# Strassen's seven products for the second feed-forward block's output too

## The chip, the cores and the metric

The kernel runs on one core of a Trainium2 chip. The core has a matrix engine (PE, TensorE; its weight loads are listed as PEld), a vector engine (DVE, VectorE), a scalar engine (ACT, ScalarE), GpSimd (POOL) and SP, which here only issues transfers (DMAs). The engines run their own instruction lists in order and wait for one another through semaphores. The metric is the time on the device in microseconds, of the whole program in one launch.

## The reference, cut to what matters

```
x = chunk_attention(q, k, v, mem_k, mem_v)         # 3072 tokens x 512
h1 = x @ moe_w_in;   g1 = h1 - tanh(h1);   y1 = g1 @ moe_w_out        # 512 -> 2048 -> 512
h2 = y1 @ moe2_w_in
g2 = maximum(h2, 0) + alpha * minimum(h2, 0)
out = g2 @ moe2_w_out                                                 # 3072 x 512, float32
```

The result is float32. Every matrix factor is split into a high part (`fp32r`, rounded) and a low part (the rest), and each product is three matmuls: high x high, high x low, low x high (`PASS` in the code).

## The kernel before, in words

**First layer.** Attention and the first feed-forward block run together, in 6 blocks of 512 tokens. In a block, for each of 16 slices `f` of the 2048 hidden units, PE makes `h` (L241), ACT takes the tanh, DVE subtracts, ACT and POOL split the result (`gh`, `gl`), and PE adds to `y` (L280). Beside this, in blocks 1 to 4 the second layer's weights are prepared ("parked"): one step per slice converts a piece of the weights from float64 to float32, forms what is needed, splits it and writes it to DRAM, to `w2i` for the inner weights and to `w2o` for the outer ones (`park_in`, `park_sum`, `park_out`). The inner weights are already parked as the seven operands of a Strassen product. The pool `w` has 34 tiles of 4 KB per partition; layer 1's own weights hold 32 of them while it runs.

**Second layer.** It runs in 3 blocks of 1024 tokens, each with an h stage and a y stage.
- The **h stage** (`pair_h`, 8 times) makes two slices of `h2` at once by Strassen's seven products in the order 1, 6, 5, 2, 7, 3, 4: 7 products x 6 matmuls of 128x512 (L368). DVE adds the products up (L385), ACT and DVE make `g2` (`prelu`: two ACT copies `n`, then one DVE instruction, L376 to L378).
- The **y stage** (`block_y`, 16 slices) is plain: `g2` is split into `g2h` and `g2l` (ACT, POOL), these are the stationary factors, the columns of `w_out` stream, and eight PSUM banks collect 8 token tiles of 128 x 512: 24 matmuls per slice, 384 per block (L445). Then the eight tiles are copied out by ACT and DVE and stored in rows of 2 KB. Each slice's weights are one load of 512 KB (`load_out`) into the space of layer 1's `ring`.
- In the y stage the next block's inputs are prepared as well (`x2_work`: 4 loads, 4 DVE sums, 7 splits).

The order on each engine is set by a scheduler from the order of the code and the tiles' dependencies. GpSimd does most subtractions that make the low parts, SP issues nearly all DMAs.

## Time and profile before

| | |
|---|---|
| median of 3 timed runs | 1111.22 us (1110.45 to 1113.46) |
| the profiled execution, first to last instruction | 1110.0 us |
| PE busy | 1082.4 us, 98% |
| DVE, ACT, POOL busy | 523.6, 478.4, 426.8 us |
| layer 2: first h stage, first y stage | 63 us and 88 us |

The profiled execution gives its span, 1110.0 us; the timed runs include what lies around the span, and their median is 1.2 us above it. Times below are microseconds from the span's start unless "mean ns" is said. An engine counts as busy while an instruction of it runs; PE runs its matmuls in a pipeline, so their pitch (start to start), not their duration, is what a matmul costs.

### The profile page before, as it was taken

Reading aid. Unit: us, or ns where it says so; the run is one execution under the profiler, and the core shown is the slowest. Engines: PE = TensorE matmul, PEld = TensorE weight load, DVE = VectorE, ACT = ScalarE, POOL = GpSimd, SP = SyncE. Lnnn points to the kernel's source line nnn. Section 1 sums busy time; section 2 is a strip of 40 time slices with the busy share of each in tenths; the row PEclk is TensorE's granted clock in tenths of the full one; section 3 lists DMA queues with packets and bytes.
Section 4 is the critical chain, followed back from the end, with each engine's and each line's share of the span. In section 5 each row is a group of like instructions: output and inputs, shape, how many; then the busy total and the mean of one; then the engine's idle time right before and its main releaser. Section 6 shows DMA issues by size and latency. Waiting matters only on the chain.

```text
span 1110.0 us, 17747 instructions
## 1 busy us (share of the span) xinstructions
PE 1082.4 (98%) x7056; PEld 892.5 (80%) x7056; DVE 523.6 (47%) x875; ACT 478.4 (43%) x789; POOL 426.8 (38%) x279
## 2 busy tenths in 40 slices
PE   4699999999999999999999999999999999999998
PEld 4588888888888888888888888888888888888887
DVE  3688754655646565564311466700566500566000
ACT  3566643443534444443332466520556420557300
POOL 3266633443434343344462000990002990003900
PEclk9699999999999999999999999999999999999999
DMA  9673234554454455335420663543754443751312
GB/s 275 258 265 115 77 124 171 164 147 166 143 176 176 154 162 170 125 148 189 176 67 1 232 214 110 180 164 106 234 194 152 152 161 129 246 175 39 110 43 76
DMA packets 57395, 171.04 MB, mean 154 GB/s; under 512 B 8288, under 2 KB 8544, under 8 KB 57312
## 3 DMA queue, kind: packets, MB, share of 16 engines
q1 hardware_dynamic: 53712, 163.48, 44.1%
q10 hardware_dynamic: 3600, 6.42, 1.6%
q8 instruction: 56, 0.92, 0.3%
q14 instruction: 27, 0.22, 0.1%
HBM read 134.23 MB, written 35.65 MB: 153 GB/s over the span
## 4 chain that ended last, share of the span: by engine, by line
PE 96%; DMA 2%; DVE 1%; issue 1%; POOL 0%; ACT 0%; SPq 0%; ACTq 0%; DVEq 0%; POOLq 0%
PE h L241 24%; PE y L280 24%; PE h L368 20%; PE yb L445 12%; PE y L445 12%; PE pv L609 2%; PE sp L525 2%; PE tp L596 1%; DMA qn<-in_q_dram 1%; DMA ri<-in_moe_w_in_dram 1%; DMA y1d<-ys 0%; PE tp L589 0%; DVE u L102 0%; SPq L495 0%; DVE s L109 0%
## 5 line engine op out<-in xcount | busy, mean ns | idle before, releaser
L241 PE MATMUL h<-ring,wt 128*128 128x512 f32 x1152 | 281.2, 392 | 4.0 <-ACT ring L616 2.2
L241 PEld LDWEIGHTS h<-ring,wt 128*128 128x128 f32 x1152 | 216.9, 189 | 50.7 <-ACT ring L616 2.4
L116 POOL TENSOR_TENSOR g2l<-g,g2h 128x1024 fp32r<-128x1024 f32 x48 | 121.7, 2570 | 282.1 <-ACT g2h L115 282.1
L368 PE MATMUL h<-xh,wi 128*128 128x512 f32 x672 | 209.0, 389 | 0.2 <-DVE g L385 0.2
L280 PE MATMUL y<-gh,wt 128*128 128x512 f32 x768 | 192.7, 391 | 0.0
L266 POOL TENSOR_TENSOR gl<-t,gh 128x512 fp32r<-128x512 f32 x96 | 126.7, 1320 | 155.3 <-ACT gh L265 129.2
L280 PEld LDWEIGHTS y<-gh,wt 128*128 128x128 f32 x768 | 143.2, 188 | 30.4
L368 PEld LDWEIGHTS h<-xh,wi 128*128 128x128 f32 x672 | 126.1, 188 | 27.0 <-DVE g L385 0.6
L257 DVE TENSOR_TENSOR t<-h,t 128x512 f32<-128x512 f32 x96 | 65.7, 685 | 153.6 <-ACT t L256 148.8
L256 ACT ACTIVATE t<-h 128x512 f32<-128x512 f32 x96 | 57.0, 594 | 130.2 <-PE h L241 118.8
L280 PE MATMUL y<-gl,wt 128*128 128x512 f32 x384 | 104.2, 389 | 0.0
L469 DVE COPY ys<-y 128x512 f32<-128x512 f32 x6 | 4.0, 688 | 198.6 <-PE y L445 198.6
L445 PE MATMUL y<-ring,g2h 128*128 128x512 f32 x384 | 96.3, 389 | 0.0
L445 PE MATMUL yb<-ring,g2h 128*128 128x512 f32 x384 | 96.1, 389 | 0.0
L445 PEld LDWEIGHTS y<-ring,g2h 128*128 128x128 f32 x384 | 72.1, 188 | 15.0
L445 PEld LDWEIGHTS yb<-ring,g2h 128*128 128x128 f32 x384 | 72.1, 188 | 15.0
L280 PEld LDWEIGHTS y<-gl,wt 128*128 128x128 f32 x384 | 72.0, 188 | 15.0
L265 ACT ACTIVATE gh<-t 128x512 fp32r<-128x512 f32 x96 | 60.5, 630 | 42.7 <-DVE t L257 34.9
L376 ACT ACTIVATE n<-g 128x512 f32<-128x512 f32 x72 | 45.4, 632 | 72.6 <-DVE g L385 72.2
L368 PE MATMUL h<-xl,wi 128*128 128x512 f32 x192 | 74.7, 389 | 0.0
L378 DVE SCALAR_TENSOR_TENSOR g<-g,n 128x512 f32<-128x512 f32 x72 | 62.7, 870 | 15.8 <-ACT n L377 14.5
L377 ACT ACTIVATE n<-n,alpha_neg 128x512 f32<-128x512 f32 x96 | 67.0, 717 | 1.3
(86 smaller groups left out, 1313.2 us busy)
## 6 DMA issues: line engine op xcount, KB each, us to landing
wi<-w2i SPq DMA_DIRECT2D x72, 512.0 KB, 4.4
ring<-w2o SPq DMA_DIRECT2D x48, 512.0 KB, 3.6
kn<-in_k_dram SPq DMA_DIRECT2D x24, 384.0 KB, 5.1
vn<-in_v_dram SPq DMA_DIRECT2D x24, 384.0 KB, 4.1
ri<-in_moe_w_in_dram SPq DMA_DIRECT2D x16, 512.0 KB, 8.3
ro<-in_moe_w_out_dram SPq DMA_DIRECT2D x16, 512.0 KB, 8.6
pk<-in_moe_w_in_dram SPq DMA_DIRECT2D x16, 512.0 KB, 3.7
w2i<-ws SPq DMA_DIRECT2D x16, 512.0 KB, 2.7
```

What stands on the lines that cost most here:

```text
L116: nc.gpsimd.tensor_tensor(out=lo, in0=v, in1=f32(hi), op=ALU.subtract)
L241: last["ffn"] = nc.tensor.matmul(out=h, lhsT=wi[:, a, kk, :], rhs=ring[c][:, s0:s0 + n, kk, :], start=(i == 0), stop=(i == 3 * KD - 1),).ins
L256: nc.scalar.activation(out=t, in_=h, func=ACTF.Tanh)
L257: last["dve"] = nc.vector.tensor_tensor(out=t, in0=h, in1=t, op=ALU.subtract).ins
L265: nc.scalar.activation(out=gh, in_=t, func=ACTF.Copy)
L266: nc.gpsimd.tensor_tensor(out=gl, in0=t, in1=f32(gh), op=ALU.subtract)
L280: mm = nc.tensor.matmul(out=yp[l, b][j][:, :n * 128], lhsT=wo[:, a, j * 128:(j + 1) * 128], rhs=g[c], start=first, stop=final,)
L368: nc.tensor.matmul(out=h, lhsT=w[:, a, 128 * kt:128 * kt + 128], rhs=x[c][:, kt, :], start=(first and j == 0), stop=(j == 5), skip_group_c ...
L376: nc.scalar.activation(out=n, in_=h, func=ACTF.Relu, scale=-1.0)
L377: nc.scalar.activation(out=n, in_=n, func=ACTF.Copy, scale=alpha_neg[:, f:f + 1])
L378: nc.vector.scalar_tensor_tensor(out=t, in0=h, scalar=0.0, in1=n, op0=ALU.max, op1=ALU.add)
L445: nc.tensor.matmul(out=sets[k][j], lhsT=g[a][:, k, j * 128:(j + 1) * 128], rhs=w[:, c, :], start=(f == 0 and n == 0), stop=(f == NF - 1 an ...
```

## The change

The y stage is made by Strassen's seven products too. Tokens are halved (512 and 512), the hidden units are paired (slices 2p and 2p+1), and the 512 output columns are halved. `w_out` becomes the stationary factor and `g2` streams, so that the products give the output transposed: 128 output columns x 512 tokens in a bank.

- **Parking**: `w_out` is parked as seven operands (`w2o[m]`), columns permuted so that a transpose by 32x32 blocks puts them right. Per pair there are two new sum steps on DVE (`park_out_sum`), and 256 KB stores instead of 512 KB ones.
- **h stage**: after the third result of a pair POOL makes two differences (`t3`, and one in place).
- **y stage**: 7 products x 8 pairs of 6 matmuls (L496 of the changed kernel). `prep` makes one streaming operand: an ACT copy to `fp32r` (L475) and a subtraction on POOL or DVE (L477); product 6 has a DVE sum ahead and one behind. `y_product` issues the matmuls, `y_done` adds the products up and, for four of the seven, transposes 32x32 blocks on DVE and stores 4 x 128 KB in pieces of 256 bytes (128 bytes for the last). The weights of a pair of products are one load of 512 KB, 28 per block instead of 16, in a pool of four tiles that takes the place of `ring`.
- The next block's inputs are prepared later in the y stage.

The diff's core:

```diff
-    w2o = [dr_p.tile([128, 2 * 512], FP32, name=f"w2o{i}") for i in range(NF)]
+    w2o = {m: [dr_p.tile([128, 2 * 2 * 256], FP32, name=f"w2o{m}_{i}") for i in range(NF // 4)]
+           for m in range(1, 8)}
...
+        v = aw.tile([128, 512], FP32, tag="v", name="wv")
+        v = to_f32(raw, v)
+        w = raw.bitcast(FP32R).rearrange("k (a s n) -> k a s n", a=2, s=2)
+        p, odd = divmod(f, 2)
+        sw[odd] = v
+        for k, m in enumerate((2, 4) if odd else (1,)):
+            split_f32(by_column(v[:, 256 * k:256 * k + 256]), by_tile(w[:, 0, k]), by_tile(w[:, 1, k]))
+            park_op(m, p, w[:, :, k])
...
+        s = t_p.tile([128, 512], FP32, tag="t", name="sm")
+        lo, hi = by_tile(s[:, 0:256]), by_tile(s[:, 256:512])
+        if half == 0:
+            nc.vector.tensor_tensor(out=hi, in0=v01, in1=v11, op=ALU.add)
+            nc.vector.tensor_tensor(out=lo, in0=hi, in1=v00, op=ALU.subtract)
+            sw["s2"] = lo
+        else:
+            nc.vector.tensor_tensor(out=lo, in0=v00, in1=v01, op=ALU.subtract)
+            nc.vector.tensor_tensor(out=hi, in0=v10, in1=sw["s2"], op=ALU.subtract)
+        w = w_p.tile([128, 2, 512], FP32R, tag="w", name="ws")
+        split_f32(s, w[:, 0], w[:, 1])
+        for k, m in enumerate((6, 5) if half == 0 else (7, 3)):
+            park_op(m, p, w[:, :, 256 * k:256 * k + 256])
...
+        mi, pp = divmod(i % NO, P2 // 2)
+        w = zr.tile([128, 2, 2, 256], FP32R, tag="wo", name="wo")
+        nc.sync.dma_start(out=f32(w).rearrange("k p a n -> k (p a n)"), in_=w2o[ORDER[mi]][pp])
+        wo2[i] = w
...
+        x = gx[b, p] = w_p.tile([128, 2, 512], FP32, tag="w", name="gx")
+        y = gy[b, p] = w_p.tile([128, 2, 512], FP32, tag="w", name="gy")
+        if p % 2 == 0:
+            t3[b, p // 2] = zr.tile([128, 2, 512], FP32, tag="t3", name="t3")
+        d3 = t3[b, p // 2][:, p % 2]
+        ga, gb = (x[:, 0], y[:, 0]), (y[:, 1], x[:, 1])
...
+        nc.gpsimd.tensor_tensor(out=d3, in0=gb[1], in1=ga[1], op=ALU.subtract)
+        nc.gpsimd.tensor_tensor(out=ga[1], in0=ga[1], in1=ga[0], op=ALU.subtract)
...
+    def y_bank(b, m):
+        if (b % 2 == 0) == (m in (1, 6)):
+            return ps_y.tile([128, 512], FP32, tag="y", name="yb")
+        if m in (1, 5):
+            return ps_h.tile([128, 512], FP32, tag="h", name="yb")
+        return ps_h2.tile([128, 512], FP32, tag="h2", name="yb")
+
+    def prep(b, s):
+        mi, p = divmod(s, P2)
+        m = ORDER[mi]
+        x, y, d3 = gx[b, p], gy[b, p], t3[b, p // 2][:, p % 2]
+        op = w_p.tile([128, 2, 512], FP32R, tag="w", name="go")
+        if m == 6:
+            src = y_bank(b, 7)
+            nc.vector.tensor_tensor(out=src, in0=d3, in1=x[:, 0], op=ALU.add)
+        else:
+            src = {1: x[:, 0], 5: y[:, 0], 2: y[:, 1], 7: d3, 3: x[:, 1], 4: x[:, 0]}[m]
+        nc.scalar.activation(out=op[:, 0], in_=src, func=ACTF.Copy)
+        eng = nc.gpsimd if m == 1 or (m != 6 and p % 4 == 3) else nc.vector
+        eng.tensor_tensor(out=op[:, 1], in0=src, in1=f32(op[:, 0]), op=ALU.subtract)
+        if m == 6:
+            nc.vector.tensor_tensor(out=x[:, 0], in0=y[:, 1], in1=src, op=ALU.subtract)
+        gop[b, s] = op
...
+    def y_product(b, s, tiles=(0, 1)):
+        mi, p = divmod(s, P2)
+        m = ORDER[mi]
+        into = {2: 1, 3: 5, 4: 7}.get(m, m)
+        if m == into and p == 0 and 0 in tiles:
+            yd[b, m] = [y_bank(b, m) for _ in range(2)]
+        w = wo2[b * NO + mi * (P2 // 2) + p // 2][:, p % 2]
+        w = w.rearrange("k a (i n) -> k a i n", i=2)
+        op = gop[b, s]
+        for i in tiles:
+            for n, (a, c) in enumerate(PASS):
                 nc.tensor.matmul(
+                    out=yd[b, into][i], lhsT=w[:, a, i], rhs=op[:, c],
+                    start=(m == into and p == 0 and n == 0), stop=(p == P2 - 1 and n == 2),
+                    skip_group_check=True,
                 )
+
+    def y_done(b, m, tiles=(0, 1)):
+        add = lambda o, p, q: nc.vector.tensor_tensor(out=o, in0=p, in1=q, op=ALU.add)
+        if m in (1, 6, 5):
+            for i in tiles:
+                tag = "gl" if m == 6 else "gh"
+                e = ye[b, m, i] = g_p.tile([128, 512], FP32, tag=tag, name="ye")
+                if m == 1:
+                    nc.scalar.activation(out=e, in_=yd[b, 1][i], func=ACTF.Copy)
+                else:
+                    add(e, yd[b, m][i], ye[b, 1 if m == 6 else 6, i])
             return
+        into, h, t, u = {2: (1, 0, 0, 0), 7: (7, 1, 1, 5), 3: (5, 0, 1, 6), 4: (7, 1, 0, 6)}[m]
+        if 0 in tiles:
+            ye[b, "st"] = w_p.tile([128, 16, 2, 32], FP32, tag="w", name="st")
+        st = ye[b, "st"]
+        for i in tiles:
+            src = yd[b, into][i]
+            if u:
+                c = t_p.tile([128, 512], FP32, tag="t", name="c")
+                add(c, src, ye[b, u, i])
+                src = c
+            nc.vector.transpose(out=st[:, :, i], in_=src.rearrange("k (b n) -> k b n", n=32))
+        t0 = 1024 * b + 512 * t
+        split = len(tiles) == 1
+        for a in range(4):
+            dst = out[t0:t0 + 512, 256 * h + 64 * a:256 * h + 64 * a + 64]
+            dst = dst.rearrange("(b i) (e j) -> i b e j", i=32, e=2)
+            src = st[32 * a:32 * a + 32]
+            if split:
+                dst, src = dst[:, :, tiles[0]], src[:, :, tiles[0]]
+            (nc.scalar if split and a % 2 else nc.sync).dma_start(out=dst, in_=src)
...
+            for s in range(LEAD):
+                prep(b, s)
+            for s in range(7 * P2):
+                if s + LEAD < 7 * P2:
+                    prep(b, s + LEAD)
+                if more or s < 6 * P2:
+                    y_product(b, s)
+                    if s % P2 == P2 - 1:
+                        y_done(b, ORDER[s // P2])
+                    i = b * NO + s // 2 + 4
+                    if s % 2 and i < NB * NO:
+                        load_out(i)
+                if s >= 2 * P2 and s % 2 == 0 and early:
+                    early.pop(0)()
+                if s >= 4 * P2 and late:
+                    late.pop(0)()
+            if not more:
+                for i in range(2):
+                    for p in range(P2):
+                        y_product(b, 6 * P2 + p, (i,))
+                    y_done(b, 4, (i,))
```

How the instructions stand, at three places. **ACT at the end of the first h stage and the start of the y stage, before** (`g_6829` and `g_6830` belong to the last pair; `g2h` is the first y operand):

```order
L376 ACTIVATE n<-h_6831 128x512
L377 ACTIVATE n<-n,alpha_neg 128x512
L115 ACTIVATE g2h<-g_6242 128x1024
L115 ACTIVATE g2h<-g_6243 128x1024
L376 ACTIVATE n<-g_6830 128x512
```

Here one Relu copy and one alpha copy of the last pair stand ahead of the first y operand, a copy of twice the width. The same place on ACT now (`go` is a y operand, made from `gx`; `yb` is a PSUM bank with the sum for product 6; L407 and L408 are `prelu`):

```order
L407 ACTIVATE n<-h_7017 128x512
L407 ACTIVATE n<-gx 128x512
L408 ACTIVATE n<-n,alpha_neg 128x512 x2
L475 ACTIVATE go<-gx 128x512 x8
L475 ACTIVATE go<-yb 128x512
L407 ACTIVATE n<-gy 128x512 x2
L475 ACTIVATE go<-yb 128x512
L408 ACTIVATE n<-n,alpha_neg 128x512 x2
L475 ACTIVATE go<-yb 128x512 x4
```

The first operand copy moved from behind one `n`, alpha copy to behind two of each, and all eight copies for product 1 stand ahead of the first for product 6.

**DVE at the same place now** (L472 is the sum ahead of product 6, L477 the low part of an operand, L479 the difference behind; before, only the last pair's L385 and L378 and four L344 stood here):

```order
L416 TENSOR_TENSOR gy<-h_7054,hu 128x512
L472 TENSOR_TENSOR yb<-t_6408,gx 128x512
L477 TENSOR_TENSOR go<-yb,go 128x512
L479 TENSOR_TENSOR gx<-gy,yb 128x512
L472 TENSOR_TENSOR yb<-t_6607,gx 128x512
L477 TENSOR_TENSOR go<-yb,go 128x512
L479 TENSOR_TENSOR gx<-gy,yb 128x512
L409 SCALAR_TENSOR_TENSOR gy<-gy,n 128x512 x2
```

Up to the last low part for product 6 this goes on in the same manner, 23 DVE instructions from the first L477 of these rows. On POOL eight L477 for product 1 stand in a row, where eight `g2l` of twice the size were mixed with the input splits.

**SP in the first y stage now** (`wo` is a weight tile for two products, `wi` a weight tile of the next h stage, `out_dram` the stores; before, the eight stores of a block stood together at its end):

```order
L353 DMA wo<-w2o_3_116 128x1024
L532 DMA out_dram<-st 32x16x64 x4
L353 DMA wo<-w2o_0_97 128x1024
L361 DMA wi_7546<-w2i_81 128x1024
L361 DMA wi_7557<-w2i_81 128x1024
L361 DMA wi_7570<-w2i_81 128x1024
L353 DMA wo<-w2o_1_98 128x1024
```

Sets of four stores now stand between the weight loads, four sets in each block.

## Rows read from the trace of the kernel before

**Rows 1.** The page's part 1: busy time, share, instructions of each engine.
```profile
PE 1082.4 (98%) x7056; PEld 892.5 (80%) x7056; DVE 523.6 (47%) x875; ACT 478.4 (43%) x789; POOL 426.8 (38%) x279
```

**Rows 2.** Busy time by stage: PE, PEld, DVE, ACT, POOL, granted clock, DMA share, GB/s.
```profile
328.00:424.00 96.00, 96.00 (x778) 78.90 (x778) 55.82 (x106) 42.59 (x78) 39.81 (x33) 1.00 0.49 164
628.40:691.50 63.10, 63.05 (x277) 51.99 (x278) 40.20 (x62) 41.21 (x64) 0.31 (x1) 1.00 0.51 163
691.50:779.90 88.40, 88.40 (x391) 73.19 (x391) 22.41 (x12) 26.66 (x32) 59.26 (x23) 1.00 0.46 155
```

**Rows 3.** The chain that ended last: start, length, what.
```profile
741.82 2.72 PE y L445 x12
...
779.90 74.80 PE h L368 x330
```

**Rows 4.** Groups by line, shapes apart: busy, mean ns of one, idle before.
```profile
L445 PE MATMUL y<-ring,g2h 128*128 128x512 f32 x384 | 96.3, 389 | 0.0
L445 PE MATMUL yb<-ring,g2h 128*128 128x512 f32 x384 | 96.1, 389 | 0.0
L445 PE MATMUL y<-ring,g2l 128*128 128x512 f32 x192 | 52.6, 389 | 0.0
L445 PE MATMUL yb<-ring,g2l 128*128 128x512 f32 x192 | 52.0, 389 | 0.0
L570 DVE STREAM_TRANSPOSE et<-sc 128x512 f32<-128x512 f32 x20 | 14.2, 710 | 23.1 <-POOL sc L563 23.0
```

**Rows 5.** Timelines of ACT, PE, DVE, POOL: start, length, instruction.
```profile
688.80 0.60 ACT L376 ACTIVATE n<-h 128x512 f32<-128x512 f32 x1
690.80 0.68 DVE L385 TENSOR_TENSOR g<-h,hv 128x512 f32<-128x512 f32 x1
691.33 0.85 PE L445 MATMUL y<-ring,g2h 128*128 128x512 f32 x3
691.96 1.14 ACT L376 ACTIVATE n<-g 128x512 f32<-128x512 f32 x2
...
434.18 1.29 POOL L266 TENSOR_TENSOR gl<-t,gh 128x512 fp32r<-128x512 f32 x1
435.43 1.29 POOL L116 TENSOR_TENSOR pk<-wv,pk 128x512 fp32r<-128x512 f32 x1
```

**Rows 6.** Timeline of DVE and POOL in the first y stage.
```profile
708.75 3.42 DVE L344 TENSOR_TENSOR xt<-x,x 128x1024 f32<-128x1024 f32 x1
...
717.73 2.40 POOL L116 TENSOR_TENSOR g2l<-g,g2h 128x1024 fp32r<-128x1024 f32 x1
```

**Rows 7.** One tile's instructions, ns min/median/max: `xt` whole run, `g` first h stage.
```profile
L344 DVE TENSOR_TENSOR xt<-x,x x6: 1215/2424/3423, 539.4 to 871.1; 128x1024 f32<-128x1024 f32 x6
...
L378 DVE SCALAR_TENSOR_TENSOR g<-g,n x21: 682/692/694, 629.0 to 688.7; 128x512 f32<-128x512 f32 x21
```

**Rows 8.** DMA issues by line, whole run: count, KB each, median us to landing.
```profile
ring<-w2o SPq DMA_DIRECT2D x48, 512.0 KB, 3.6
```

**Rows 9.** DMA queue: packets, MB, share of 16 engines; 233.3 to 234.1, then 1106 to 1110.
```profile
q1 hardware_dynamic: 1286, 0.01, 90.1%
...
q1 hardware_dynamic: 547, 0.86, 56.6%
```

**Rows 10.** Timeline of the end: the last matmul, the last copies, the last issue.
```profile
1105.91 0.39 PE L445 MATMUL yb<-ring,g2l 128*128 128x512 f32 x1
1106.34 0.38 ACT L461 ACTIVATE ys<-yb 128x256 f32<-128x256 f32 x1
1106.75 0.42 DVE L463 COPY ys<-yb 128x256 f32<-128x256 f32 x1 [1.08 <-ACT ys L461]
1107.20 0.33 SPq L464 DMA_DIRECT2D out_dram<-ys  x1
```

**Rows 11.** Groups by line: two of the four DVE sums of the parked inner weights, layer 1.
```profile
L158 DVE TENSOR_TENSOR sm<-wv,sm 128x256 f32<-128x256 f32 x8 | 11.0, 1377 | 0.0
...
L153 DVE TENSOR_TENSOR sm<-wv 128x256 f32<-128x256 f32 x8 | 5.1, 639 | 1.0 <-DMA y1d<-ys 0.9
```

More of the change, by code (lines that the diff above doesn't have):

```diff
@@ L69, in chunk_attention_two_ffn_kernel @@
     w_p = ctx.enter_context(tc.tile_pool(name="w", bufs=2 * NF + 2))
-    x_p = ctx.enter_context(tc.tile_pool(name="x", bufs=1))
+    xstack = ExitStack()
+    x_p = xstack.enter_context(tc.tile_pool(name="x", bufs=1, side="right"))
     t_p = ctx.enter_context(tc.tile_pool(name="t", bufs=4))
@@ new lines, in park_out, with park_out_sum @@
+        p, odd = divmod(f, 2)
[3 more added lines that the diff above has]
+            park_op(m, p, w[:, :, k])
+    def park_out_sum(p, half):
+        (v00, v01), (v10, v11) = [[by_column(sw[j][:, 256 * k:256 * k + 256]) for k in range(2)] for j in range(2)]
+        s = t_p.tile([128, 512], FP32, tag="t", name="sm")
[11 more added lines that the diff above has]
+            park_op(m, p, w[:, :, 256 * k:256 * k + 256])
@@ L386, in pair_h @@
         d = {}
-        for j in range(2):
-            g2[b, f + j] = w_p.tile([128, 2, 512], FP32, tag="w", name="g2")
-        ga, gb = [[g2[b, f + j][:, k] for k in range(2)] for j in range(2)]
+        x = gx[b, p] = w_p.tile([128, 2, 512], FP32, tag="w", name="gx")
[4 more added lines that the diff above has]
+        ga, gb = (x[:, 0], y[:, 0]), (y[:, 1], x[:, 1])
         def bank(m):
-            if b > 0:
+            if b % 2:
                 t = ps_y.tile([128, 512], FP32, tag="y", name="h2")
@@ L420, in pair_h @@
         prelu(gb[0], gb[0], f + 1)
-    def split_g2(b, f):
-        hi = w_p.tile([128, 2, 512], FP32R, tag="w", name="g2h")
-        lo = w_p.tile([128, 2, 512], FP32R, tag="w", name="g2l")
-        split_f32(g2.pop((b, f)), hi, lo)
-        gsp[b, f] = (hi, lo)
-    def block_y(b, f):
-        if f == 0:
-            sets = [[ps_y.tile([128, 512], FP32, tag="y", name="y") for _ in range(4)], [
-                pool.tile([128, 512], FP32, tag=tag, name="yb")
-                for pool, tag in ((ps_h, "h"), (ps_h2, "h2")) for _ in range(2)]]
-            yp[1, b] = sets
-        sets = yp[1, b]
-        g = gsp.pop((b, f))
-        w = wo2.pop(b * NF + f)
-        halves = (1, 0) if f == 0 and b > 0 else (0, 1)
-        end = f == NF - 1 and b == NB - 1
-        for k in halves:
-            steps = [(n, j) for n in range(3) for j in range(4)]
-            if end:
-                steps.sort(key=lambda x: x[1])
-            for n, j in steps:
-                a, c = PASS[n]
+    def y_bank(b, m):
[4 more added lines that the diff above has]
+        return ps_h2.tile([128, 512], FP32, tag="h2", name="yb")
@@ L445, in block_y @@
+    yd = {}
+    ye = {}
+    def y_product(b, s, tiles=(0, 1)):
[9 more added lines that the diff above has]
+            for n, (a, c) in enumerate(PASS):
                 nc.tensor.matmul(
-                    out=sets[k][j], lhsT=g[a][:, k, j * 128:(j + 1) * 128], rhs=w[:, c, :],
@@ L769, in chunk_attention_two_ffn_kernel @@
                     nc.sync.dma_start(out=alpha_sb, in_=alpha.rearrange("(k p) -> p k", p=128))
-            if 0 < b < N1 - 1:
-                park_step((b - 1) * NF + f)
+            if (b == 0 and f == NF - 1) or 0 < b < N1 - 1:
+                next(park)()
             if b == N1 - 1:
@@ L781, in chunk_attention_two_ffn_kernel @@
                     work = x2_work(0) + [lambda q=q: load_in(0, q) for q in range(4)]
-                    early = [g for g in range(8) if (g % 4) // 2 != x0[0][b] // 4]
                     for q in range(4):
                         load_in(1, q)
-                    wait_for = [g for g in range(8) if g not in early]
                 for _ in range(2):
@@ L788, in chunk_attention_two_ffn_kernel @@
                         work.pop(0)()
-                if f == 12:
-                    for g in early:
-                        load_out(g)
             if i + 1 < len(slots):
@@ L797, in chunk_attention_two_ffn_kernel @@
                     work.pop(0)()
+                xstack.close()
+                zr = ctx.enter_context(tc.tile_pool(name="zr", bufs=4, side="right"))
                 pair_h(0)
-                for g in wait_for:
+                for g in range(4):
                     load_out(g)
```

127 lines of the change are left out of this document (42 added, 85 removed).

## The prediction

> **What bounds the kernel now.** The share of each engine comes first: PE is busy for 1082.4 of 1110.0 us, no other engine for half of it [rows 1]. The table by stage says where that holds: in a stretch of layer 1 with parking PE is busy 96.00 of 96.00 us beside DVE's 55.82, in the first h stage 63.05 of 63.10, in the first y stage 88.40 of 88.40 [rows 2]. The chain that ended last is then almost all PE, and its rows give the price of a matmul: 12 of them in 2.72 us are 226.7 ns each, and 330 h matmuls in 74.80 us again 226.7 [rows 3]. The four groups of y matmuls show idle time of 0.0 ahead of them [rows 4]. So in layer 2 a matmul removed is 0.2267 us gained, and any wait that PE gets is lost in full.
>
> **The gain.** Before, a block's y stage has 384 matmuls (the four groups hold 384 + 384 + 192 + 192 = 1152 for three blocks). Now it has 7 products x 8 pairs x 6 = 336 of the same shape, 128x128 against 512 columns. 3 x 48 = 144 fewer, times 0.2267: **-32.6 us**. That swapped factors keep the pitch follows from y and h having the same one, though their stationary and streaming sides hold different things; the granted clock was 1.00 in all these stretches [rows 2].
>
> **From h to y.** Here the cover gets thinner. Before, PE goes from h to y without idle time: the last copies of the last pair start on ACT at 688.80, and the first y matmul at 691.33 finds an operand that was split long ago [rows 5]. Now the first operand copy stands behind two Relu and two alpha copies (the second order listing). Four at about 0.6 us from 688.80 end near 691.2, the operand copy 0.6 later; with handoffs it is some 0.8 us after the end of h. POOL then takes 1.29 for the low part (a 128x512 subtraction, pitch 1.25 [rows 5]): 2.1 us. Only two matmuls (0.45) can run before a low part is wanted, so PE loses 1.6. After that PE wants a low part every 6 x 0.2267 = 1.36 us and POOL gives one every 1.25, unless DVE holds it up.
>
> It does: when DVE and POOL run together they stretch each other. `xt` takes 1215 ns at its fastest and 3423 at its slowest [rows 7]; the one of 3.42 us in the y stage is about a POOL `g2l` (2.40) longer than the fastest [rows 6]. This looks like one engine waiting out a whole instruction of the other. [...] Beside the eight POOL splits DVE now runs such instructions (the second halves of `prelu`, 692 ns [rows 7], and sums for product 6), so I add 0.7: 2.3 us in blocks 0 and 2. In block 1 four spare PSUM banks let the sums start sooner and an alpha copy stands later on ACT; I take 0.7 there. Together **+5.3**; 0 if all is hidden, 12 if the next step fails too.
>
> **Product 6** has the longest preparation: a sum, a low part and a difference on DVE for each of eight pairs. Its ACT copies stand behind the eight for product 1: 0.6 + 7 x 0.51 (the pitch of a pair of 128x512 copies of 1.14 us [rows 5]) after 0.8, so the first low part is done near 5.0. Behind it are 23 DVE instructions at a pitch near 0.60, 13.8 us, and some 3.5 us of waits for POOL: the last is ready at 22.3. PE wants it after 15 products and two matmuls, 15 x 1.36 + 0.45 + 2.3 = 23.2. It fits by about 1 us. At full durations (0.69 each, handoffs uncovered) it is late by almost 5 us in blocks 0 and 2 and 2 in block 1: that is rival B.
>
> **Later in the y stage** an operand costs ACT 0.6 and DVE or POOL 0.7 to 1.29 per 1.36 us of PE, and preparation runs many products ahead: 0. In the **h stage** POOL is idle (0.31 of 63.10 us [rows 2]); two differences of 1.25 per 9.5 us pair fit: 0.
>
> **Weights.** 512 KB land in 3.6 us [rows 8], now 28 times per block instead of 16, one per two products (2.72 us). Each is issued three tiles ahead, 3 x 2.72 = 8.2 us, so 4.6 us of slack remain: 0, while nothing else delays the queue.
>
> **Stores.** A set is 4 x 128 KB in pieces of 256 bytes, 2048 packets. The trace has none of that size. The nearest: 1286 packets of 4 bytes held 16 engines at 90.1% for 0.8 us, 9 ns each per engine; 547 packets of about 1.57 KB held them at 56.6% for 4 us, 66 ns each [rows 9]. By interpolation a 256-byte packet takes 9 + 256 x 57/1572 = 18 ns, a set 2048 x 18 / 16 = 2.3 us, inside the 4.6 of slack. At 66 ns it is 8.4 us, and the weights behind it come 3.8 late. I take the interpolation, as 256 lies nearer to 4 than to 1572; 66 ns is rival C. [...]
>
> **The tail.** Now 3.7 us lie between the end of the last matmul (1106.30) and the end of the span (1110.0): a copy on ACT and one on DVE (0.42), an issue, a landing [rows 10]. After the change a sum (0.69) and a 32x32 transpose (0.71 [rows 4]) replace the copies: +0.5. Two issues of 0.33 on each of two queues add 0.4. Four times 512 packets of 128 bytes at an interpolated 13.7 ns take 1.75 us for some 0.8: +1.0. **+2.0**, between 0.9 (packets hidden) and 8.5 (66 ns).
>
> **Layer 1.** Parking gets four more 128x256 DVE sums per pair of slices. Such sums take 639 to 1377 ns here [rows 11], so about 4 us per pair, 30 in all; POOL gets about 2 us more per pair. The stretch of [rows 2] has 40 us of 96 free on DVE and 56 on POOL, and PE is full although the same kind of sums is already there. I take 0.06 us per new step, **+1**; 0 if it is hidden and 16 x 1.4 = 22 if every step's longest sum delays PE.
>
> **Sum**: 1110.0 - 32.6 + 5.3 + 2.0 + 1 = 1085.7 for the span; the median lay 1.2 above this execution's span, so **1087 us**.
>
> **Rivals.**
> - **B, the DVE chain is late.** Product 6 costs PE nearly 5 us in blocks 0 and 2 and 2 in block 1: 12 in place of 5.3, so about 1094; with the tail or the stores at half their upper bound up to 1102. For it: the margin is 1 us on a count of 23 instructions. Against it: the pitch of 0.60 where instructions stand in a row. 0.17.
> - **C, slow stores; the other side.** Past the slack a set stalls PE by 128 x t - 4.6 us (t in us per packet), 11 sets that matter (the last is in the tail). What is left of the gain without it, 1111.2 - 1087 = 24, is used up at 2.2 us per set, t = 53 ns. At 66 ns: 3.8 x 11 = 42 us, and with the tail about 1130 to 1136: slower. For it: the one row with full-size packets is at 66 ns, and no row lies between. Against it: that packet is six times as large. Slower 0.07, and 0.03 for a partial stall that ends at 1103 to 1110.
> - **D, parking holds up layer 1**, by half its upper bound, 11 us: 1097. For it: DVE queues behind POOL there (639 against 1377 ns for like sums [rows 11]); against it: PE's full 96.00. 0.06.
> - **E, the transition is hidden**: low parts are early enough, and only part of the tail is paid: 1111.2 - 32.6 + 1 to 2, 1079 to 1081. 0.07.
>
> **How the numbers follow.** My forecast, 1081 to 1092, has 0.6, B 0.17, C 0.10, D 0.06, E 0.07. Two runs of this kernel can be told apart from about 0.3%, 3.3 us. Everything but C is faster than 1108, and so is two thirds of C's partial stall: faster 0.91, same 0.02, slower 0.07. The range from 1080 to 1102 leaves out C, a part of E and the upper end of B and D, some 0.17.
>
> **What would show it.** PE's y groups should count 1008 matmuls at a pitch of 226.7 ns. Right for the transition: idle time of PE ahead of the first y products, released by POOL's low parts, 1 to 3 us in the first and third block, and none ahead of product 6. If product 6 shows idle time released by DVE, B holds. Weights' landings should stay below 8 us and PE should never be released by a weight load; if it is, right behind a set of stores, C holds. In layer 1, PE full as in [rows 2] shows parking hidden, and the time from the last matmul to the end should be near 5.7 us. The forecast is wrong altogether if the pitch of the matmuls is not 226.7, or if DVE and POOL slow each other beyond 0.7 us per block also where operands are prepared far ahead.

## The result, and the profile after

The changed kernel takes 1119.39 us (median of 4 runs, 1117.42 to 1120.95); the kernel before took 1110.84 beside it. The ratio is 1.0071, 95% interval 1.0051 to 1.0091: **0.7% slower**, where 1087 us were forecast. The profiled execution has a span of 1118.8 us, 8.8 above the one of before.

The page's busy times after, to be held against [rows 1]:

```profile
PE 1075.2 (96%) x6912; PEld 867.5 (78%) x6912; DVE 693.6 (62%) x1111; ACT 523.4 (47%) x926; POOL 480.4 (43%) x357
```

144 instructions are gone from PE, as counted, but its busy time fell by 7.2 us and not by 32.6. PE is still busy for 96% of the span, so most of what is missing is not idle time: some matmuls must have become dearer. Pieces of the chain that ended last (start, length, what) show it:

```profile
220.26 6.39 DMA w2i<-ws
226.72 3.56 DMA pk<-in_moe_w_out_dram
...
361.88 2.73 PE y L308 x12
364.61 2.80 PE h L269 x12
...
652.12 62.89 PE h L399 x276
...
785.08 8.39 PE yb L496 x36
```

The 36 y matmuls at 785.08 take 8.39 us, a pitch of 233.1 ns against 226.7 [rows 3]. The h stage (L399) keeps its pitch, 62.89 / 276 = 227.9. And layer 1, whose code for PE is unchanged, ends 23.7 us later, as the same 276 matmuls of the first h stage show in the chain of the kernel before, and DMAs of the parking now stand in the chain:

```profile
628.45 63.04 PE h L368 x276
```

The h matmuls of layer 1 (L269) have a pitch of 2.80 / 12 = 233.3 ns too, the y matmuls beside them 227.5. The groups by line and shape (busy, mean of one | idle time before; the first line is of the kernel before, the others of the changed one):

```profile
L241 PE MATMUL h<-ring,wt 128*128 128x512 f32 x1152 | 281.2, 392 | 4.0 <-ACT ring L616 2.2 <-DVE ring L617 1.8
...
L269 PE MATMUL h<-ring,wt 128*128 128x512 f32 x1152 | 290.6, 401 | 8.3 <-DVE t L285 3.6 <-ACT ring L672 2.7 <-DVE ring L673 2.1
L496 PE MATMUL yb<-go,wo 128*128 128x512 f32 x1008 | 239.7, 396 | 4.3 <-DMA wo<-w2o 1.8 <-POOL go L477 1.7 <-ACT go L475 0.6
...
L308 PE MATMUL y<-gh,wt 128*128 128x512 f32 x768 | 194.1, 394 | 4.7 <-ACT gh L293 4.7
```

L269 stands at 401 ns, where the same matmuls (L241) stood at 392, and L496 at 396, where each form of the y matmuls stood at 389 [rows 4]. The two slow forms have one thing in common: they read a tile from the right-hand side of the memory (`ring`, `wo`), where the change moved `ring` to and put `wo`. L308 has 4.7 us of idle time that was not there, and L269 3.6 us behind DVE; its waits for `ring` were there before. By stage (columns as in [rows 2]; here the same stretch of layer 1 and the first y stage, with some h matmuls of the next block in it):

```profile
328.00:424.00 96.00, 93.38 (x752) 75.09 (x751) 58.84 (x114) 43.81 (x83) 44.17 (x38) 1.00 0.50 166
717.70:804.90 87.20, 84.42 (x357) 66.36 (x357) 72.30 (x77) 41.55 (x70) 51.91 (x27) 1.00 0.74 234
```

PE was full in the first of these and is now idle for 2.6 of 96 us, though DVE has only 3 us more to do there than in [rows 2]. What it waits for can be followed once, in the timeline of the changed kernel (start, length, engine, instruction, and in brackets the idle time before it and its releaser):

```profile
218.93 0.33 SPq L93 DMA_DIRECT2D pk<-in_moe_w_out_dram  x1
219.35 0.38 SPq L565 DMA_DIRECT2D vn<-in_v_dram  x1
...
219.83 0.38 SPq L558 DMA_DIRECT2D qn<-in_q_dram  x1
220.26 0.42 SPq L166 DMA_DIRECT2D w2i<-ws  x1
...
226.72 0.33 SPq L93 DMA_DIRECT2D pk<-in_moe_w_out_dram  x1
...
230.31 0.62 ACT L101 ACTIVATE u<-pk 128x512 f32<-128x512 f32 x1 [3.08 <-DMA pk<-in_moe_w_out_dram]
...
231.53 2.11 PE L308 MATMUL y<-gh,wt 128*128 128x512 f32 x8 [1.36 <-ACT gh L293]
```

`pk` (raw weights to be parked) and `ws` (a parked sum) share the two tiles of the pool `w` that layer 1's weights leave free. The store of a `ws` is issued at 220.26, behind a load of `pk` that had to wait for the other tile and behind two token loads; it lands 6.4 us later; only then the next `pk` load starts, 226.72; ACT stands at `u<-pk` until 230.31 with layer 1's own `gh` behind it, and PE waits for that `gh`. The waits of ACT for these loads from 215 to 640 us, after the change:

```profile
ACT u L101 <- DMA pk<-in_moe_w_out_dram: 34.1, 9, 6.5
...
ACT u L101 <- DMA pk<-in_moe_w_in_dram: 21.4, 7, 4.4
```

and in the kernel before:

```profile
ACT u L99 <- DMA pk<-in_moe_w_out_dram: 17.5, 5, 4.3
...
ACT u L99 <- DMA pk<-in_moe_w_in_dram: 6.4, 3, 2.8
```

55.5 us in 16 waits against 23.9 in 8. SP's own waits say what holds the `pk` loads back, first after and then before (us in total, times, longest): it stands longest for the stores that leave from `ws`.

```profile
SPq L93 <- DMA w2i<-ws: 61.7, 16, 6.3
```

```profile
SPq L91 <- DMA w2i<-ws: 39.6, 13, 5.3
```

### The profile page after: what moved, and what is told of

It is laid out like the page before. It is cut to its first block, busy times and chain, and to the rows that moved or that the text cites. A ratio compares the mean times of both kernels' runs of the same rounds, so it can differ in the third digit from the quotient of the medians.

```text
span 1118.8 us, 18224 instructions
## 1 busy us (share of the span) xinstructions
PE 1075.2 (96%) x6912; PEld 867.5 (78%) x6912; DVE 693.6 (62%) x1111; ACT 523.4 (47%) x926; POOL 480.4 (43%) x357
## 3 DMA queue, kind: packets, MB, share of 16 engines
q1 hardware_dynamic: 93712, 188.52, 52.4%
## 4 chain that ended last, share of the span: by engine, by line
PE 69%; issue 9%; DVE 7%; DMA 6%; POOL 4%; ACT 2%; SPq 1%; POOLq 0%; ACTq 0%; DVEq 0%
PE h L269 20%; PE y L308 19%; PE yb L496 16%; PE h L399 10%; DMA w2i<-ws 2%; PE pv L665 2%; DVE go L477 2%; POOL gy L453 1%; PE sp L581 1%; DMA pk<-in_moe_w_out_dram 1%; POOL t L452 1%; DMA qn<-in_q_dram 1%; ACT go L475 1%; PE tp L652 1%; DMA pk<-in_moe_w_in_dram 1%
## 5 line engine op out<-in xcount | busy, mean ns | idle before, releaser
L269 PE MATMUL h<-ring,wt 128*128 128x512 f32 x1152 | 290.6, 401 | 8.3 <-DVE t L285 3.6
L269 PEld LDWEIGHTS h<-ring,wt 128*128 128x128 f32 x1152 | 218.2, 190 | 62.1 <-DVE t L285 4.9
L496 PE MATMUL yb<-go,wo 128*128 128x512 f32 x1008 | 239.7, 396 | 4.3 <-DMA wo<-w2o 1.8
L496 PEld LDWEIGHTS yb<-go,wo 128*128 128x128 f32 x1008 | 187.8, 187 | 55.4 <-POOL go L477 6.5
L399 PE MATMUL h<-xh,wi 128*128 128x512 f32 x672 | 208.8, 389 | 1.2 <-DVE gx L409 1.2
L308 PE MATMUL y<-gh,wt 128*128 128x512 f32 x768 | 194.1, 394 | 4.7 <-ACT gh L293 4.7
L308 PEld LDWEIGHTS y<-gh,wt 128*128 128x128 f32 x768 | 143.1, 188 | 38.5 <-ACT gh L293 6.0
L399 PEld LDWEIGHTS h<-xh,wi 128*128 128x128 f32 x672 | 126.1, 188 | 28.1 <-DVE gx L409 1.6
L452 POOL TENSOR_TENSOR t<-gx,gy 128x512 f32<-128x512 f32 x24 | 32.3, 1347 | 174.0 <-DVE gy L409 166.4
L308 PE MATMUL y<-gl,wt 128*128 128x512 f32 x384 | 104.3, 392 | 0.0
L308 PEld LDWEIGHTS y<-gl,wt 128*128 128x128 f32 x384 | 72.6, 189 | 15.5
L104 DVE TENSOR_SCALAR u<-u 128x512 uint32<-128x512 uint32 x64 | 44.3, 696 | 51.1 <-ACT u L101 51.0
L399 PE MATMUL h<-xl,wi 128*128 128x512 f32 x192 | 74.7, 389 | 0.0
L477 POOL TENSOR_TENSOR go<-gx,go 128x512 fp32r<-128x512 f32 x36 | 56.6, 1596 | 24.7 <-ACT go L475 24.7
L408 ACT ACTIVATE n<-n,alpha_neg 128x512 f32<-128x512 f32 x96 | 66.6, 717 | 1.0
L475 ACT ACTIVATE go<-gx 128x512 fp32r<-128x512 f32 x72 | 41.5, 622 | 38.0 <-PE yb L496 22.9
L118 POOL TENSOR_TENSOR wt<-s,wt 128x512 fp32r<-128x512 f32 x32 | 41.3, 1292 | 41.3 <-ACT wt L117 40.9
L399 PE MATMUL h<-x,wi 128*128 128x512 f32 x144 | 56.0, 389 | 0.0
```

The costliest lines, as they stand in the source:

```text
L104: nc.vector.tensor_scalar(out=u, in0=u, scalar1=3, scalar2=None, op0=ALU.logical_shift_left)
L269: last["ffn"] = nc.tensor.matmul(out=h, lhsT=wi[:, a, kk, :], rhs=ring[c][:, s0:s0 + n, kk, :], start=(i == 0), stop=(i == 3 * KD - 1),).ins
L308: mm = nc.tensor.matmul(out=yp[l, b][j][:, :n * 128], lhsT=wo[:, a, j * 128:(j + 1) * 128], rhs=g[c], start=first, stop=final,)
L399: nc.tensor.matmul(out=h, lhsT=w[:, a, 128 * kt:128 * kt + 128], rhs=x[c][:, kt, :], start=(first and j == 0), stop=(j == 5), skip_group_c ...
L408: nc.scalar.activation(out=n, in_=n, func=ACTF.Copy, scale=alpha_neg[:, f:f + 1])
L475: nc.scalar.activation(out=op[:, 0], in_=src, func=ACTF.Copy)
```

## The experiments

Theory at the start: two faults that have nothing to do with the product count. **A**: where `ring` and `wo` start in the memory makes their matmuls slower. **T**: the spare tiles of the parking come back too late. Rivals: **R**, the pitch follows from traffic beside PE; **D**, the DVE sums of the parking hold up layer 1, as in the prediction's rival D. Times below are medians, ratios are to the kernel before on the same chip.

**1. `e1_aligned`.** An unused tile ahead of `ring`; every engine's instructions and their order stay.

```diff
+    pad = ctx.enter_context(tc.tile_pool(name="pad", bufs=1, side="right")).tile([128, 8], FP32, name="pad")
     xstack = ExitStack()
```

> The changed kernel with one unused tile of 32 bytes per partition ahead of the layer-1 ring, so that the ring, the wo tiles and t3 start at multiples of 64 bytes (in the changed kernel they start 32 bytes beside one); the instructions and their order on every engine are the same. Theory A (the start of a tile sets the pitch): the matmuls that read these tiles, L269 (1152, ring streams) and L496 (1008, wo is stationary), go from about 233 ns back to 226.7, together 2160 x 6.5 ns = 14 us: span near 1105. Rival R (the longer pitch comes from the heavier DMA traffic or from DVE and POOL reading beside PE): pitch stays at 233, time within 0.3% of the changed kernel's 1119.

Measured 1114.85 us, 1.0032 (1.0017 to 1.0047). The chain of e1, y and h matmuls:

```profile
361.96 2.80 PE h L269 x12
...
783.35 8.24 PE yb L496 x36
```

L496 went from 233.1 to 229.0 ns with nothing changed but a place; that speaks for A and against R. L269 did not move at all, so the theory's number, 64 bytes, was wrong.

**2. `e2_before_off32`.** The kernel before with `ring` alone moved by 32 bytes (and what lies behind it by 64).

```diff
+    pad = x_p.tile([128, 8], FP32, name="pad")
     ring = [x_p.tile([128, RING, KD, 128], FP32R, name=f"ring{i}") for i in range(2)]
+    pad2 = x_p.tile([128, 8], FP32, name="pad2")
```

> The kernel before with the ring alone moved by 32 bytes; all other tiles keep their place to 64 bytes. Theory A: the 1152 L241 and 1152 L445 matmuls that stream from the ring take 233 ns instead of 226.7: +15 us, near 1126. Rival R: no change, 1111.

Measured 1133.46 us, 1.0204 (1.0182 to 1.0225): +22 us from 64 bytes of padding. Its chain:

```profile
192.09 2.79 PE h L241 x12
...
718.24 2.80 PE y L445 x12
...
796.64 76.36 PE h L368 x330
```

Both forms that stream from `ring` went to 233, as A said. The 7 us above its forecast are L368 (231.4 ns against 226.7: half of its weights lie in a pool behind the ring, 64 bytes off) and L280 (12 in 2.75 to 2.76 us, its streaming `gh` and `gl` lie 64 bytes off). This is R's end as the cause of the pitch: the kernel before has neither new traffic nor new DVE work.

**3. `e3_no_dve_sums` and `e4_no_ws_store`.** On e1: the sums' DVE work left out, or their stores.

```diff
     def park_out_sum(p, half):
...
-            nc.vector.tensor_tensor(out=hi, in0=v01, in1=v11, op=ALU.add)
-            nc.vector.tensor_tensor(out=lo, in0=hi, in1=v00, op=ALU.subtract)
...
+        s = sw[half]
```

and e4, with the operands of products 1, 2 and 4 loaded for the others:

```diff
         for k, m in enumerate((6, 5) if half == 0 else (7, 3)):
-            park_op(m, p, w[:, :, 256 * k:256 * k + 256])
+            pass
```

> As e1_aligned, and park_out_sum leaves out its four DVE sums (the operands for products 6, 5, 7 and 3 are copies of the unsummed weights, so the output is another); its tile, ACT copy, POOL subtraction and stores stay. Theory T (layer 1 loses its time because two spare tiles must take eight loads or stores per pair in turn, and ACT waits for the next load): PE's idle time in layer 1, about 10 us in the changed kernel, stays within 3 us of e1's. Rival D (rival D of the prediction: the sums on DVE hold up layer 1): idle time falls to about 0 and the time is 12 to 16 us below e1.

> As e1_aligned, and park_out_sum issues no stores (layer 2 loads the operands of products 1, 2 and 4 in their place, so the output is another); its sums, ACT copy and POOL subtraction stay. Theory T: the tile of a sum is free as soon as POOL is done, so most of layer 1's idle time goes: 8 to 16 us below e1. Rival D: no change against e1.

e3 took 1117.59 us, 1.0057 (1.0040 to 1.0073); e4 1104.10, 0.9928 (0.9908 to 0.9948). Busy time of PE in the 400 us from 220 to 620, all layer 1 with parking, in e1, e3 and e4, in this order:

```profile
220.00:620.00 400.00, 392.74 (x2754) 316.36 (x2754) 207.73 (x381) 167.57 (x308) 177.44 (x144) 0.99 0.46 151
```

```profile
220.00:620.00 400.00, 391.33 (x2743) 314.00 (x2742) 182.26 (x353) 166.92 (x308) 174.14 (x144) 0.99 0.46 149
```

```profile
220.00:620.00 400.00, 398.61 (x2797) 322.54 (x2797) 210.45 (x383) 170.26 (x312) 178.58 (x146) 1.00 0.39 132
```

The kernel before has 400.00 there, the changed one 390.71. With 25 us of DVE work gone PE waits as in e1 (8.7 us against 7.3); with the stores gone and all DVE work kept, 1.4 us are left. D falls, T stands.

**4. `e5_align128`.** The pad of e1 with 24 elements in place of 8.

> The changed kernel with 96 unused bytes per partition ahead of the ring instead of 32, so that ring and wo start at multiples of 128 bytes (in e1_aligned at odd multiples of 64); order unchanged. In e1_aligned the pitch of L496 fell from 233.1 to 229.0 ns, that of L269 stayed at 233.3. Theory A2 (what counts is the place of a tile within 128 bytes; the streaming side pays 6.6 ns for any offset, the stationary side 2.3 at 64 and 6.4 at 32): both go to 226.7, 1152 x 6.6 + 1008 x 2.3 = 10 us below e1, near 1105. Rival R2 (the ring's matmuls are slow for where the ring now lies, at the top of the memory, or for the traffic beside them): L269 stays at 233.3 and the time within 2 us of e1's 1114.9.

Measured 1118.08 us, 1.0049 (1.0030 to 1.0068): A2 falls. L496 even went back up:

```profile
68.20 2.79 PE h L269 x12
...
782.83 8.37 PE yb L496 x36
```

**5. `e6_early_prep`.** On e5, part of the transition from h to y moved ahead of the last pair.

```diff
+                if p == P2 - 1:
+                    for s in range(4):
+                        prep(b, s)
                 if i > 0:
                     pair_h(i)
...
-            for s in range(LEAD):
+            for s in range(4, LEAD):
```

> As e5, and the first four operands of product 1 are prepared ahead of the last pair of each h stage instead of behind it. Theory B (what the y stages lose at their start is the wait for the copies and POOL splits behind the last pair): the waits of the first L496 go, 3 blocks x 1 to 2 us, and the whole is 3 to 5 us below e5. Rival S (the y stage's start is limited by the chain on DVE for product 6, not by product 1): the first waits go but come back as idle time ahead of product 6; within 1.5 us of e5.

1117.40 us, 1.0050 (1.0035 to 1.0065): no gain, as S said. PE's waits for POOL's low parts (1.7 us in e5) are gone, those for ACT's copies rose from 0.6 to 2.4. That is S only in part: 0.4 us each stand ahead of product 6 in two blocks, 1.5 ahead of product 5 in the other, and none is released by DVE. PE is also idle for 3 us more in layer 1, which the edit doesn't touch (389.48 of 400 us busy against 392.58), so that this run alone could hide a gain; e12 below tries the edit without that fault.

**6. `e7_act_stores` and `e8_v_tiles`.** On e5, two remedies for the late tiles: the sums' stores from ACT's queue, or fewer uses of the tiles. e7, in `park_sum` (and for the stores of `park_out_sum` alike):

```diff
-        nc.sync.dma_start(out=w2i[p][:, c:c + 1024], in_=f32(w))
+        nc.scalar.dma_start(out=w2i[p][:, c:c + 1024], in_=f32(w))
```

e8, in `park_sum` (the same in `park_out_sum`, with `sw[0]` and `sw[1]`):

```diff
+        if half:
+            split_f32(s, v0.bitcast(FP32R), v1.bitcast(FP32R))
+            nc.sync.dma_start(out=w2i[p][:, c:c + 512], in_=v0)
+            nc.sync.dma_start(out=w2i[p][:, c + 512:c + 1024], in_=v1)
+            return
         w = w_p.tile([128, 1024], FP32R, tag="w", name="ws")
...
```

> As e5, and the stores of the parked sums are issued by ACT, not by SP behind its token loads. Theory T1 (the spare tiles come back late because the stores stand in SP's queue behind a load that itself waits for a tile, and then behind 0.5 MB token loads): waits of ACT for the pk loads (58 us in the changed kernel) fall by half or more and layer 1 gains 6 to 12 us against e5. Rival T2 (two tiles are too few for eight uses per pair wherever the stores stand, or ACT's in-order wait for POOL costs as much): within 3 us of e5 or slower.

> As e5, and the second sum of each kind (in and out) writes its split into the two wv tiles, which are free by then, so that a pair needs six spare-tile uses instead of eight, as many as in the kernel before; four stores instead of one or two leave from there. Theory T: ACT's waits for the pk loads fall to near the 24 us of the kernel before and layer 1 gains 8 to 14 us against e5. Rival: the wv tile is now the one that comes back late, DVE waits for it, and the gain is under 4 us.

e7: 1110.80 us, 0.9998 (0.9985 to 1.0010), 7.3 below e5. e8: 1106.00, 0.9948 (0.9928 to 0.9967), 12.1 below e5. PE in e8, from 220 to 620 us, and then ACT's waits from 215 to 640:

```profile
220.00:620.00 400.00, 399.78 (x2805) 324.58 (x2804) 209.57 (x381) 170.00 (x310) 179.95 (x146) 1.00 0.45 148
```

```profile
ACT u L101 <- DMA pk<-in_moe_w_in_dram: 8.3, 3, 2.8
...
ACT u L101 <- DMA pk<-in_moe_w_out_dram: 5.1, 3, 1.8
```

The same sums, splits and stored bytes, two tile uses fewer per pair: the waits fall from 52.4 us (e5) to 13.4, and SP's waits for `w2i<-ws` from 60.0 to 13.9. The tiles are the cause. What the queue adds is small: in e7 PE is still busy for only 394.25 of these 400 us, against 392.58 in e5. From its first matmul to its last, layer 1 is 2.8 us shorter in e7 than in e5 (592.1 against 594.9) and 10.8 in e8 (584.1). Most of e7's 7.3 us lies elsewhere in the profiled executions: 2.1 us ahead of the first matmul and 2.0 in the first y stage, where 12 y matmuls of the chain take 4.58 us in e5 (at 774.14, behind a wait of 2.7 us for weights) and 3.03 in e7 (at 768.37). The edit touches neither place.

**7. `e9_align256` and `e10_before_all32`.** The pad with 56 elements (224 bytes); and the kernel before with 32 bytes ahead of nearly everything.

```diff
+    pad = const.tile([128, 8], FP32, name="pad")
     alpha_sb = const.tile([128, NF], FP32, name="alpha_sb")
```

> The changed kernel with 224 unused bytes ahead of the ring: ring and wo start at multiples of 256 bytes, as every tile of the kernel before does and as no version of the changed kernel so far did (they stood 224, 192 and 128 bytes past one). Order unchanged. Theory A3 (streaming and stationary operand must stand at the same place within 256 bytes): L269 and L496 both at 226.7 ns, 1152 x 6.6 + 1008 x 6.4 = 14 us below the changed kernel's 1119, near 1105. Rival R2 (the place of the ring at the top of the memory, or traffic): pitch still near 233, time 1115 to 1119.

> The kernel before with 32 unused bytes ahead of nearly all its tiles, so that both operands of every large matmul stand 32 bytes past a multiple of 256. Theory A3 in its relative form (the difference of the two operands counts): pitch stays 226.7, time 1111. In its absolute form (each operand has to start at a multiple of 256): all large matmuls rise towards 233 and more, 6,900 x 6.5 ns = 45 us or more, 1156 and above.

e9's chain has the old pitch in both forms:

```profile
262.26 2.72 PE h L269 x12
...
781.34 8.16 PE yb L496 x36
```

and e10 takes 1112.45 us, 1.0003 (0.9993 to 1.0013), with

```profile
780.36 74.80 PE h L368 x330
...
1030.60 2.72 PE y L445 x12
```

So no operand needs a place of its own: what counts is how far the two operands of a matmul stand apart within 256 bytes. (The absolute form would have cost about 29 us, not the 45 expected: the kernel has 4464 large matmuls, not 6,900. The measured time excludes both.) The places below are those of the built programs, the pitches from the chains above and of the changed kernel:

| streaming minus stationary, mod 256 | seen in | ns per matmul |
|---|---|---|
| 0 | before, e9, e10 | 226.7 |
| 32 | L496 changed; L445, L241 e2 | 233 |
| 64 | L496 e1; L280 e2 | 229 to 230 |
| 128 | L269, L496 e5 | 232.5 |
| 192 | L269 e1 | 233.3 |
| 224 | L269 changed | 233 |

(The L368 of e2, half of them at 192, fit this less well: their mean of 231.4 would mean 236 for that half.) That the count goes by 256 is read from pairs: within 512 bytes the operands of L496 in the changed kernel, e1 and e5 stand 288, 320 and 384 apart, and they have the pitch of the matmuls that stand 32, 64 and 128 apart (L445 and L280 of e2, L269 of e5). All the fast cases are multiples of 512; a distance of 256 itself was not run.

But e9's time is 1113.07 us, 1.0013 (0.9993 to 1.0033), 6 below the changed kernel and not 14. PE's 220 to 620 us says one part of why; it is busy for the least of all:

```profile
220.00:620.00 400.00, 386.42 (x2758) 314.71 (x2757) 206.63 (x381) 167.78 (x309) 176.92 (x144) 1.00 0.47 153
```

In layer 1 the faster PE waits longer for the same parking, 13.6 us against 9.3. The other part is the first y stage: there PE waits 2.6 us once for weights, and the 12 y matmuls behind the wait take 4.46 us in the chain (at 772.78), where 12 at 226.7 ns take 2.72, so that the stage is 0.9 us longer than in the changed kernel in spite of the pitch.

**8. `e11_align256_v_tiles` and `e12_all_three`.** Both remedies, and both with the edit of e6.

> e9 and the edit of e8_v_tiles together. If the two causes are separate, their gains add up: 14 us for the places and 12 for the tiles (e8 against e5, 1106.0 against 1118.1) below the changed kernel's 1119, near 1093, 1.7% faster than the kernel before. If they share one wait (a faster PE waits longer for the parked weights), less: 1098 or more.

> e11 and the edit of e6_early_prep. In e6 the waits for product 1 went and others came in their place, 0.7 us below e5: within 2 us of e11. If with the faster pitch the start of the y stages is the next limit, 3 us below e11.

e11: 1093.93 us, 0.9840 (0.9822 to 0.9858); e12: 1095.02, 0.9846 (0.9832 to 0.9861). With both faults gone the change is 1.6% faster than the kernel before. The early preparation gives nothing here either.

**9. `e13_late_stores` and `e14_spread_x2`.** What e11 still loses in its first y stage. Its stretches there:

```profile
744.00:748.00 4.00, 4.00 (x20) 3.30 (x18) 4.00 (x7) 0.63 (x1) 0.19 (x1) 1.00 0.00 0
748.00:752.00 4.00, 2.88 (x13) 2.06 (x11) 2.31 (x5) 0.83 (x2) 0.00 (x0) 1.00 0.75 202
752.00:756.00 4.00, 2.35 (x9) 1.92 (x10) 3.77 (x6) 3.38 (x5) 3.18 (x2) 0.89 1.02 410
756.00:760.00 4.00, 4.00 (x14) 3.17 (x13) 1.22 (x1) 1.40 (x3) 4.00 (x3) 0.69 1.05 385
```

No byte moves from 744 to 748 us; then PE is idle for 2.8 us, and after that the granted clock is 0.89 and 0.69. DVE, SP and PE in e11's timeline:

```profile
745.86 1.30 DVE L535 STREAM_TRANSPOSE st<-yb 128x512 f32<-128x512 f32 x2
747.19 2.05 SPq L544 DMA_DIRECT2D out_dram<-st  x4
749.33 0.49 SPq L365 DMA_DIRECT2D wo<-w2o  x1
...
753.64 4.24 PE L508 MATMUL yb<-go,wo 128*128 128x512 f32 x12 [2.77 <-DMA wo<-w2o]
```

SP stood at a set of stores that waited for DVE's transposes, and the weights queued behind it. e13 issues a set later, counted down once per product:

```diff
-        for a in range(4):
+        def store():
+          for a in range(4):
...
+        if split:
+            store()
+        else:
+            put.append([6, store])
...
+                    for x in put:
+                        x[0] -= 1
+                    while put and put[0][0] <= 0:
+                        put.pop(0)[1]()
...
+            while put:
+                put.pop(0)[1]()
```

e14 also spreads the x2 loads:

```diff
-                if s >= 2 * P2 and s % 2 == 0 and early:
+                if early and (s % 4 == 0 if len(early) > 4 else True) and s >= 2 * P2:
                     early.pop(0)()
```

> e11, and each set of stores (not the last of the program) is issued six products later, so that SP does not stand at a set whose transposes DVE has not done, with weight loads queued behind it. In e11's first y stage no byte moves from 744 to 748 us while SP waits, and PE then waits 2.8 us for a wo load and runs at a granted clock of 0.69 in the next stretch. Theory Q (head of SP's queue): this wait and the clock loss go, 3 to 5 us below e11's 1093.9. Rival (the 256-byte stores themselves or the total traffic delay the loads): no change, within 1.5 us.

> e13, and the four x2 loads of the next block stand four products apart instead of two. The other wait for wo in e11's first y stage (0.7 us) came behind them, a load that took 8.3 us. Theory Q: 0.5 to 1.5 us below e13. Rival: the later sums collide with the next part, no gain or slower.

e13: 1092.83 us, 0.9837 (0.9818 to 0.9855), no difference to e11 that can be measured: the scheduler put the first set where it was, still ahead of a weight load, and PE waits 2.0 us there. e14: 1090.04, 0.9802 (0.9788 to 0.9815). In its first y stage one run of 250 matmuls has no listed gap:

```profile
695.88 58.15 PE L509 MATMUL yb<-go,wo 128*128 128x512 f32 x250 [0.62 <-POOL go L489]
```

With the loads, and the four long DVE sums that follow them, further apart, SP stands at the first set of stores for 2.8 us (743.50 to 746.28), where in e11 it was 6.8 (740.35 to 747.19), and no weights are late. Whether e14 needs e13's edit at all was not tried apart.

## Why the prediction was wrong

Its sum, term by term, for the changed kernel's profiled execution:

| term | forecast | measured |
|---|---|---|
| 144 matmuls removed | -32.6 | -32.6 (1008 in place of 1152, at 226.7) |
| pitch of the others | 0 | +14.1 (1152 x 6.6 + 1008 x 6.4 ns) |
| waits in the y stages | +5.3 | +8.2 |
| tail | +2.0 | +1.7 |
| layer 1 beside the pitch | +1 | +16.1 (23.7 - 7.6) |
| sum | -24.3 | +7.5, of +8.8 between the spans |

**The gain: wrong.** The step that failed is "that swapped factors keep the pitch follows from y and h having the same one". The forms agreed in the kernel before because the operands of all its large matmuls lie at one place within 256 bytes. The same fault, in a term that the sum did not have, made the 1152 L269 of layer 1 dearer. The change moved `ring` to the other side of the memory, which I read as a matter of space. That the sides are not what counts is shown by e2 (left side, slow) and e9 (right side, fast). The prediction had named a pitch other than 226.7 as what would make it wrong altogether.

**Layer 1: wrong, and by most.** The step was "PE is full although the same kind of sums is already there. I take 0.06 us per new step". Full was right for before; the sums on DVE were harmless (e3). What I priced was DVE's and POOL's work, and not the two tiles and the loads and stores that a step takes in turn: eight uses per pair where there were six. Rival D had the right place with the wrong mechanism and too small a price, 11 us. With six uses (e8) PE is idle for 0.2 of 400 us. The 16.1 us can be divided further: 10.5 are idle time (432.10 us from 220 to the end of layer 1, 421.61 busy), 0.7 lie ahead of the first matmul (47.8 against 47.0), and about 3.4 are clock: the granted clock was 0.50 from 239.67 to 243.08 and from 434.23 to 437.64, 6.8 us of which half is counted as lost (an estimate from e11, where matmuls start 0.43 us apart in such a stretch and 0.227 before it). The rest, 1.5 us, was not followed.

**From h to y: mechanism right, size smaller, the rest elsewhere.** The first y matmul of the changed kernel starts 0.3 us after the end of the first h stage and the first low part releases PE after 1.7, where 0.8 and 2.1 were forecast; the listed waits are 0.9 us at that start. No run shows the 0.7 us that the forecast added in blocks 0 and 2 for DVE beside POOL. What the changed kernel shows in its place is a POOL slower than the forecast's 1.25 us: its first eight low parts take 12.96 us, 1.62 each (the L409 of DVE beside the first takes 1.80 us, where the like of it took 0.69 [rows 7]), and PE, which wants one every 1.4, falls behind by 0.2 us more at each of the next two products. With these gaps the three starts cost 4.3 us, against 5.3. Product 6 costs nothing that the profile lists: rival B did not happen. Its last low part is done at 739.7, 22.0 us after the h stage; the forecast had 22.3, and the 3.5 us of waits for POOL in it were an estimate that no run shows apart. The y stages lose 8.2 us in all (243.2 us from the ends of the h stages to the last y matmuls, without the h matmuls between, less 1008 x 233.1 ns): 4.1 in listed waits, 1.8 of these for weights, the rest in gaps inside the runs of matmuls. The slack of 4.6 us for weights was conditioned on "nothing else delays the queue", and something did: x2 loads, and stores that wait for DVE (e11, e14). One landing of weights took 9.4 us, where all were to stay below 8.

**Stores: right.** In the stretch with one set of stores alone (from 1105 to 1111 us) and with the last ones (from 1115 to 1118), the queues of the changed kernel hold (packets, MB, share of 16 engines):

```profile
q1 hardware_dynamic: 2151, 0.62, 40.8%
```

```profile
q10 hardware_dynamic: 1056, 0.13, 27.3%
q1 hardware_dynamic: 1056, 0.13, 27.0%
```

6 x 16 x 0.408 / 2151 = 18.2 ns is the mean of the first, in which 23 packets of 4 KB are counted; the 2048 packets of 256 bytes alone took 17.0. 3 x 16 x 0.543 / 2112 = 12.3 ns per packet of the second, nearly all of 128 bytes. Interpolation had given 18 and 13.7. (Its 66 ns were a mean as well: the packets there have 1 KB, 46 ns, and 2 KB, 84 ns.) Rival C is excluded: a set would have stalled the weights from 4.6 / 128 = 36 ns on. Its sign did appear: at 777.96 PE waits 1.5 us for weights that stood behind a set of stores. But SP issued these stores only at 771.96, when the transposes were done (770.63 and 1.30 us more), so they were late and not slow. Per KB the small pieces are the dearer ones, 17.0 ns for 256 bytes being 66 per KB where the packets of [rows 9] took 42, but here that time was hidden.

**Tail: right.** From the last matmul's end (1113.4) to the end of the span (1118.8) are 5.4 us; 5.7 were forecast. The last steps on DVE:

```profile
1113.44 0.69 DVE L503 TENSOR_TENSOR c<-yb,ye 128x512 f32<-128x512 f32 x1 [1.12 <-PE yb L496]
1114.16 0.71 DVE L523 STREAM_TRANSPOSE st<-c 128x512 f32<-128x512 f32 x1
```

The forecast of 1087 us comes close to the change without its two faults: e14, with them and the crowd of loads removed, takes 1090. (By its own chances "faster" adds up to 0.92, not 0.91.)

## What to carry to other kernels

When an edit moves or adds a tile that matmuls read, compute where it starts relative to the other operand before taking the old pitch: a pad of 224 bytes was worth 6 us alone, and 12 against a pad of 96 where nothing else held PE (e8 to e11). When work is added to a step that runs "in the shadow", count the buffers that it turns over, with load and store in each turn, and not only the engines' time; of two faults in one stretch one can hide part of the other's remedy (e9), so try remedies together as well as apart. Before a load is put behind a store in a queue, ask what the store waits for: in e11 SP stood 6.8 us at a set of stores that waited for DVE, the weight loads behind it were issued after it, and PE waited 2.8 us for weights.
